# A fused attention and MLP block on one core: the second half's attention moved to a written list of slots, and the attention output loaded with one DMA a tile

## The chip, the cores and the metric

The kernel runs on one core of one Trainium2 chip. The metric is device time in microseconds (us) for one execution; lower is better. A core has a matrix engine (PE, with its weight loads PEld), a vector engine (DVE), a scalar engine (ACT), a GpSimd engine (POOL) and a sync engine (SP) that here issues all DMA transfers. Each engine works through its own instructions strictly in the order of the program, and waits on semaphores for the others.

## The reference

`x` has 2048 tokens of 576 channels. The output is `x + A(LN(x)) + B(LN(x))`, all in float32:

```python
# A: 32 heads of 18 channels, window of 8 keys with stride 2
qkv = xn @ wqkv
logits = q . k[pos - 2*w] * scale        # w = 0..7, masked where pos - 2*w < 0
o = softmax(logits) . v[pos - 2*w]
A = o @ wo
# B: 576 -> 4608 -> 576
B = mish(xn @ w1 + b1) @ w2
```

## The kernel before

**Halves.** The tokens are done in two halves of 1024 (`hf` 0 and 1), of eight tiles of 128 tokens each. Each half goes through LayerNorm and transposes, the q/k/v projection (`q` items, for the second half also `z` items, which use a seven-product scheme), and 18 groups `q` of 256 hidden channels of the MLP. The products are made of float32 parts: a high and a low part of each operand and three matmuls instead of one. At the very end come eight `o` blocks (`wo_part`, L1068), which multiply the attention output of both halves with `wo`, two token tiles at a time, add the rest and store.

**The plan.** All of this is one list, `plan`, of 456 items in a fixed order: `("m", hf, q, part)` are six parts of the first MLP product, `("p", ...)` are parts of the second, `("q", ...)`, `("z", ...)`, `("o", ...)` as above. `before(i, fn)` hangs side work on item `i`: weight loads, splits, attention steps. When the program is written out, each item first emits what lies in `soon` (work that an earlier step put off by one item), then its side work in the order in which it was hung, then what an earlier item left in `pend` (the mish evaluations, L716 to L723), then its own matmuls. Every engine gets its instructions in this order; a list of dependencies at the end of the program pins it.

**One group of the first MLP product** (`m1_part`, L730 on) uses three PSUM banks. Part 3's bank is `cur[3]`: the DVE add at L716 reads it (`rt`), and part 4 then accumulates into the same bank. In the group `q = 0` the order of the parts is 0, 2, 1, 3, 5, 4, and the adds that are kept in `late` (among them `rt`) are emitted in part 5. So part 4 cannot begin before the DVE has done `rt`. In the group `q = 1` the order is 0, 2, 1, 3, then one `z` item, then 4 and 5; there too part 4 waits for an `rt` add.

**Attention** (`attention`, L518) is a generator with 73 steps a half: eight pairs of head units, nine steps a pair, and one last step. Steps 0 to 3 of a pair multiply queries with windowed keys into `pr`; the sum over a head's channels (`L543`, DVE) follows at the next step. Normally the product is done on POOL (L538); for the first pair of the second half it is done on DVE (L534). Step 4 takes the maximum (L557), subtracts it (L559) and leaves the exponential for ACT. Step 5 divides (L567 to L569), and steps 5 to 8 multiply with the values on POOL (L576) and sum on DVE (L582). The step after a pair's last one leaves `o_turn` in `soon`: a DVE transpose (L598) into `oT`, and one item later `o_send`, four SP stores into `o_d[hf]` in DRAM (L605). The first call of the generator, four items ahead of its first step, issues the loads of the first two keys and queries (L491, L500).

**Where the steps stand before.** One formula places the 146 steps of both halves: a list `marks` of places with a `rate` each gives every item a cost, the total is cut into equal parts, and each step goes to the next item that the list `ok` allows.

| step of the second half | item before |
|---|---|
| loads of the first keys and queries | 258 (`m 1 0 3`) |
| pair 0, steps 0, 1, 2, 3, 4, 5 | 262 (`m 1 1 2`), 265 (`z 3 3`), 268 (`m 1 2 0`), 271, 274, 278 |
| pair 1, steps 0 and 5 | 291, 307 |
| pair 2, steps 0 and 5 | 320, 335 |
| pair 3, step 0 | 348 |
| pair 7, steps 3 to 8, and the last step | 419, 421, 423, 425, 427, 428, 429 |

The first half's last two steps stand at items 257 and 260. Items 255 to 260 are the six parts of the group `q = 0` in the order 0, 2, 1, 3, 5, 4, items 261 to 264 the parts 0, 2, 1, 3 of `q = 1`, 265 the `z` item, 266 part 4. Item 270 is the first product with the second MLP weights (`p_item`, L861).

**The end.** `o_load` (L890) fetches a token tile of the attention output into `o`: one DMA of 256 KB for 512 channels (L894), and the remaining 64 channels twice, into the lower and the upper 64 partitions, by two DMAs (L897). Tiles 0 and 1 of the first half are loaded one item ahead of item 428 (`p 1 17 1 0`), tiles 2 and 3 at the first `o` item, 432, the others two blocks ahead of their use. `o_split` (L899) then copies and splits them with ACT (L916 to L932) and DVE (L919 on); `wo_part` calls `o_split` for the next block while it does its own.

Of the kernel before, what the change touches and what calls it, by code (L numbers as in the profile page):

```python
# [8 lines left out]
F32 = mybir.dt.float32  # L9
# [5 lines left out]
S, D, F = 2048, 576, 4608  # L15
H, DH, W, DIL = 32, 18, 8, 2
HALO = (W - 1) * DIL
P = 128
NH = 2
# [3 lines left out]
TJ = SH // P  # L23
JB = TJ // NB
KT = D // P
NF = F // P
NP = NF // 2
NQ = 4
UQ = 4
PU = 2  # L30
CU = 2 * DH
OC = 4
# [7 lines left out]
def block_kernel(ctx: ExitStack, tc: tile.TileContext, x, wq, wo, w1, b1, w2, mask, out):  # L40
    nc = tc.nc
# [5 lines left out]
    dram = ctx.enter_context(tc.tile_pool(name="dram", bufs=1, space=bass.MemoryType.DRAM))  # L47
# [548 lines left out]
    def o_turn(hf, pair, og):  # L596
        oT = sb.tile([P, PU * CU * TJ], F32, tag="oT", bufs=1, name=f"oT_{hf}_{pair}")
        nc.vector.transpose(oT, og.rearrange("p c j -> p (c j)"))  # L598
        soon.append(lambda: o_send(hf, pair, oT))

    def o_send(hf, pair, oT):
        rows = o_d[hf][pair * PU * CU:(pair + 1) * PU * CU].rearrange("(n c) j p -> (c j) n p", c=4)
        for g in range(4):
            part = slice(g * 32, (g + 1) * 32)
            nc.sync.dma_start(rows[:, :, part], oT[part].rearrange("i (n k) -> i n k", k=32))  # L605

    ASTEPS = NQ * UQ // PU * 9

# [281 lines left out]
    def o_load(hf, j):  # L890
        if j >= TJ or (hf, j) in os_:
            return
        o = os_[hf, j] = sb.tile([P, 5 * P], F32, tag="xn", bufs=XNB, name=f"o_{hf}_{j}")
        nc.sync.dma_start(o[:, 0:KT * P].rearrange("p (k t) -> p k t", k=KT),  # L894
                          o_d[hf][0:KT * P, j, :].rearrange("(k p) t -> p k t", p=P))
        for r_ in range(2):
            nc.sync.dma_start(o[r_ * 64:(r_ + 1) * 64, KT * P:], o_d[hf][KT * P:D, j, :])  # L897

    def o_split(p, step, early=False):  # L899
        hf, j = divmod(2 * p, TJ)  # L900
# [234 lines left out]

    kv_d = [dram.tile([2 * UQ, HALO + S, CU], F32, name=f"kv_d{g}") for g in range(NQ)]
    q_d = [dram.tile([UQ, S, CU], F32, name=f"q_d{g}") for g in range(NQ)]
    o_d = [dram.tile([D, TJ, P], F32, name=f"o_d{h}") for h in range(NH)]
    y_d = dram.tile([SH, D], F32, name="y_d")

    def rest_loads():
# [6 lines left out]
    at = {}  # L1148
# [7 lines left out]
    def before(i, fn):  # L1156
        plan[max(i, 0)][1].append(fn)
# [75 lines left out]
    CHUNKS = ((1, 0), (1, 1), (0, 0), (0, 1))  # L1233
# [112 lines left out]
    def spot(hf, q, i):  # L1346
        return at["s", hf, q, i]

    for q in range(NP):
        if q == 0:  # L1350
            i = at["q", 0, 3, 1, 0]
            ps_ = dict(raw=i - 3, sums=i - 1, wa=i, wc=i + 1, t0=i + 2, t1=i + 4)
        elif q == 1:
            i = at["q", 0, 3, 0, 0]
# [16 lines left out]
    for q in range(1, 2 * OC + 1):  # L1371
        i = spot(0, q, (3,2)[q > 1])
# [5 lines left out]
    i = spot(0, NP - 1, 0)  # L1378
# [5 lines left out]
    i = at["q", 1, 0, 1, 1]  # L1384
# [4 lines left out]
    i = spot(0, 9, 4)  # L1389
    for k in range(2):  # L1390
        for n, steps in enumerate((
# [4 lines left out]
            for kind, name in steps:  # L1396
                f = dict(l=z_load, s=z_sum, h=z_high, o=z_low, k=z_keep)[kind]
                d = 30 + 2 * n + (n >= 14) if k else 2 * n if n < 10 else (19, 20, 22, 23, 25, 26, 27)[n - 10]
                before(i + d, lambda f=f, name=name, k=k: f(name, k))
    for q in range(NP):  # L1400
        if q == 0:
            i = at["z", JB - 1, 0]
            ps_ = dict(wa=i - 7, t0=i - 6, t1=i - 5, wc=i - 4)
        elif q == 1:
            i = spot(1, 0, 0)
# [19 lines left out]
    for n, (a, b) in enumerate((("P6", "P1"), ("P7", "P6"), ("P6", "P5"), ("P2", "P1"), ("P3", "P6"), ("P4", "P7"), ("P5", "P7"))):  # L1425
        for pr in range(2):
            i = items[-2][2] + 1 + (0,1,2)[n] if n < 3 else at["p", 1, J + 0 - 1, n > 4, pr] + (1, 7, 1, 2)[n - 3]
# [6 lines left out]
    i = at["q", 0, 1, 1, 0]  # L1434
# [3 lines left out]
    i = at["q", 0, 3, 1, 0]  # L1438
# [5 lines left out]
    i = at["q", 1, 0, 1, 1]  # L1444
    for n in range(8):
        c, k = divmod(n, 4)
# [7 lines left out]
    for n in range(0, JB, 2):  # L1454
        i = at["q", 0, 1, 0, n]
# [4 lines left out]
    for n in range(TJ):  # L1460
        i = spot(0, 2 + n, 2)
# [3 lines left out]
    i = spot(0, NP - 2, 0)  # L1465
# [7 lines left out]
    for n, (name, pr) in enumerate((name, pr) for name in ("P4", "P5", "P2", "P3") for pr in range(2)):  # L1473
        i = items[dict(P4=0, P5=2, P3=2, P2=3)[name]][2] + pr
# [4 lines left out]
    att = {}  # L1479
    T = [0.0]  # L1480
# [1 line left out]
        T.append(T[-1] + p_[2])  # L1482

    ok = [True] * len(plan)
    for hf in range(NH):
        for q in range(1, NP):
            for i in range(10):
                ok[spot(hf, q, i)] = i in ((0, 3, 7, 9), (0, 3, 5, 7, 9))[hf] + (1,) * (hf and q >= NP - 4) and (q > 1 or i)

    for q in range(2 * OC + 2):  # L1490
        for i in range(spot(1, q, 0), spot(1, q, 9) + 1):
            ok[i] = True

    marks = [at["q", 0, 2, 0, 1], at["q", 0, 3, 0, 0], spot(0, 1, 0), spot(0, 2 * OC + 1, 0), at["q", 1, 0, 0, 0], at["z", 0, 0], spot(1, 0, 0),
             spot(1, 2, 0), spot(1, 2 * OC + 2, 0), spot(1, NP - 1, 0), at["o", 0, 0], at["o", 2, 0]]
    rate = (1.15, 0.4, 0.5, 0.8, 1.15, 1.25, 1.2, 0.8, 1.5, 0.8, 0)
    T = [0.0]
    for i in range(len(plan)):
        w = [r_ for m, r_ in zip(marks, rate) if m <= i][-1:] or [0]
        T.append(T[-1] + plan[i][2] * w[0])  # L1500
    total = T[at["o", 2, 0]]
    steps = ASTEPS + 1
    cuts = []
    k = marks[0] - 1
    for n in range(2 * steps):
        t = n * total / (2 * steps)
        if n == steps:
            k = max(k, spot(1, 0, 0) + 1)
        k = next(k for k in range(k + 1, len(plan)) if T[k + 1] > t and ok[k])
        hf = n // steps  # L1510
        if n % steps == 0:
            before(k - 4, lambda hf=hf: (att.__setitem__(hf, attention(hf)), next(att[hf])))
        before(k, lambda hf=hf: next(att[hf], None))
        cuts.append(k)

    i = spot(1, *(11,3))
    for k in range(4):
# [3 lines left out]
    for n, name in enumerate(("T3", "T1", "T2", "T4", "B11", "B21", "B22", "R", "D")):  # L1521
        k = i + 10 + (2, 5, 10, 15, 20, 25, 30, 35, 40)[n]
# [5 lines left out]
    i = spot(1, NP - 1, 0)  # L1528
# [3 lines left out]
    j = at["p", 1, NP - 1, 1, 0]  # L1532
# [2 lines left out]
        before(j + n // 2, lambda name=name: wo_fetch(name))  # L1535
    for k in range(2):
        before(j + -1, lambda k=k: o_load(0, k))
        before(at["o", 0, 0], lambda k=k: o_load(0, 2 + k))
    for k in range(4):
        before(j + (1, 1, 2, 3)[k], lambda k=k: o_split(0, k, True))  # L1540
    for p_ in range(TJ // 2):
# [1 line left out]
    for k in range(4, 2 * TJ):  # L1543
        before(at["o", k // 2 - 2, 0], lambda k=k: o_load(*divmod(k, TJ)))
# [52 lines left out]
```

## Time and profile before

| | |
|---|---|
| median of 3 runs | 1114.85 us (1114.71 to 1118.95) |
| the profiled execution | 1116.75 us |
| its span, first to last instruction | 1115.0 us |
| mean granted PE clock | 0.998 |

The profile is of one execution. A row of the timeline gives the start and the length of a piece in us, the engine, the line of the kernel, the operation, the tiles as output<-input, how many instructions are merged in it, and in brackets the idle time of the engine ahead of it with what ended that. SPq rows are DMAs as SP issues them. A row of the view of waits gives engine, tile and line that waited, what it waited for, the sum in us, how often, and the longest. A row of the view of windows gives a stretch, then for each engine the busy time and the instructions, then the granted PE clock as a share of full speed, the mean busy share of the 16 DMA engines, and GB/s.

### The profile page before, as it was taken

The page shows a single profiled execution, that of the slowest core. Times are in us where ns is not written, and L with a number is a line of the kernel's source. Part 1 is how long each engine was busy: PE and PEld are TensorE (multiplying, and loading weights), DVE is VectorE, ACT ScalarE, POOL GpSimd, SP SyncE. Part 2 cuts the span into 40 slices and gives each one's busy share as a digit, 9 for nine tenths or more (in the row PEclk, how much of TensorE's full clock was granted, in tenths as well). Part 3 has the DMA queues.
Part 4 walks back from the last instruction along what each step waited for, and adds up shares of the span by engine and source line. Part 5 has one row for each costly group of instructions (what it writes and reads, how often), then busy time and mean ns, then how long its engine had stood idle before and what let it go on. Part 6 is the DMA issues. An engine that isn't in the chain of part 4 may idle for free.

```text
span 1115.0 us, 18242 instructions
## 1 busy us (share of the span) xinstructions
PE 1102.7 (99%) x6550; PEld 1015.9 (91%) x6550; DVE 846.0 (76%) x1371; ACT 499.2 (45%) x917; POOL 777.4 (70%) x631
## 2 busy tenths in 40 slices
PE   8999999999999999999999999999999999999998
PEld 7999899999999999999999889988899999998898
DVE  6369788888889888897666576686775677877776
ACT  5544645544554534555232355353342443444253
POOL 2479777767679687785787336666779878877532
PEclk9999999999999999999999999999999999999999
DMA  6899695868767858666697797764665567777474
GB/s 204 281 313 312 229 350 214 293 225 282 260 239 268 272 200 310 245 234 215 190 332 254 230 351 268 238 215 161 217 224 180 193 209 238 278 254 238 138 227 143
DMA packets 174558, 271.08 MB, mean 243 GB/s; under 512 B 49506, under 2 KB 116356, under 8 KB 174468
## 3 DMA queue, kind: packets, MB, share of 16 engines
q1 hardware_dynamic: 174468, 269.91, 71.3%
q8 instruction: 52, 0.85, 0.3%
q14 instruction: 38, 0.31, 0.1%
HBM read 160.39 MB, written 109.48 MB: 242 GB/s over the span
## 4 chain that ended last, share of the span: by engine, by line
PE 87%; POOL 6%; DVE 3%; issue 1%; ACT 1%; DMA 1%; SPq 1%; POOLq 0%; DVEq 0%; ACTq 0%
PE h L671 28%; PE po L769 21%; PE pq L348 9%; PE po L882 9%; PE po L861 7%; PE h L677 5%; PE o L1068 5%; PE z L446 3%; POOL pv L576 2%; POOL act L723 1%; POOL pr L538 1%; POOL s L622 1%; DVE u L815 1%; POOL accP L870 1%; PE ta L75 0%
## 5 line engine op out<-in xcount | busy, mean ns | idle before, releaser
L769 PEld LDWEIGHTS po<-w,act 128*128 128x128 f32 x1728 | 236.4, 188 | 6.0 <-POOL act L723 0.4
L769 PE MATMUL po<-w,act 128*128 128x288 f32 x1728 | 240.7, 295 | 0.1
L576 POOL TENSOR_TENSOR pv<-L,kv 128x576 f32<-128x576 f32 x128 | 177.2, 1482 | 40.6 <-DVE L L569 31.1
L538 POOL TENSOR_TENSOR pr<-q,kv 128x576 f32<-128x576 f32 x120 | 184.6, 1564 | 6.9 <-DMA q<-q_d 5.1
L723 POOL TENSOR_TENSOR act<-c,act 128x512 fp32r<-128x512 f32 x81 | 107.6, 1329 | 114.2 <-ACT act L722 110.9
L773 DVE TENSOR_TENSOR acc<-po,acc 128x288 f32<-128x288 f32 x288 | 119.5, 449 | 29.6 <-PE po L769 28.8
L348 PE MATMUL pq<-wq,xt 128*128 128x432 f32 x672 | 136.4, 361 | 1.0 <-ACT xt L81 0.9
L882 PEld LDWEIGHTS po<-w,act 128*128 128x128 f32 x960 | 130.9, 188 | 5.2 <-DVE accP L885 2.1
L882 PE MATMUL po<-w,act 128*128 128x288 f32 x960 | 133.6, 295 | 1.5 <-DVE accP L885 1.4
L348 PEld LDWEIGHTS pq<-wq,xt 128*128 128x128 f32 x672 | 125.0, 188 | 7.9 <-ACT xt L81 1.5
L717 ACT ACTIVATE c<-c,b1c 128x512 f32<-128x512 f32 x81 | 58.7, 725 | 144.7 <-DVE c L716 144.5
L671 PE MATMUL h<-xt,t 128*128 128x512 f32 x432 | 110.5, 391 | 0.2 <-DVE rt L716 0.2
L671 PE MATMUL h<-S,t 128*128 128x512 f32 x432 | 110.4, 391 | 0.0
L582 DVE TENSOR_REDUCE og<-pv 128x144 f32<-128x1152 f32 x64 | 86.1, 1346 | 29.8 <-POOL pv L576 29.8
L671 PE MATMUL h<-xt,wa 128*128 128x512 f32 x432 | 104.1, 390 | 0.0
L543 DVE TENSOR_REDUCE L<-pr 128x64 f32<-128x1152 f32 x64 | 85.8, 1343 | 23.1 <-POOL pr L538 23.0
L705 ACT COPY c<-h 128x512 f32<-128x512 f32 x81 | 47.5, 586 | 119.2 <-PE h L677 65.8
L671 PEld LDWEIGHTS h<-xt,wa 128*128 128x128 f32 x432 | 80.9, 188 | 17.0
L861 PEld LDWEIGHTS po<-pw,u 128*128 128x128 f32 x672 | 92.1, 188 | 4.4 <-DVE u L815 1.8
L861 PE MATMUL po<-pw,u 128*128 128x288 f32 x672 | 94.1, 295 | 1.4 <-DVE u L815 1.4
L671 PEld LDWEIGHTS h<-xt,t 128*128 128x128 f32 x432 | 79.0, 188 | 15.1 <-DVE rt L716 0.6
L671 PEld LDWEIGHTS h<-S,t 128*128 128x128 f32 x432 | 77.9, 188 | 12.8
(229 smaller groups left out, 1842.9 us busy)
## 6 DMA issues: line engine op xcount, KB each, us to landing
kv<-kv_d SPq DMA_DIRECT2D x64, 396.0 KB, 5.2
kept_t<-t SPq DMA_DIRECT2D x36, 512.0 KB, 4.8
t<-kept_t SPq DMA_DIRECT2D x36, 512.0 KB, 4.7
rw<-in_w SPq DMA_DIRECT2D x36, 320.0 KB, 4.6
kept_wa<-wa SPq DMA_DIRECT2D x18, 640.0 KB, 4.6
kept_w<-w SPq DMA_DIRECT2D x20, 576.0 KB, 4.2
wa<-kept_wa SPq DMA_DIRECT2D x18, 640.0 KB, 4.8
w<-kept_w SPq DMA_DIRECT2D x20, 576.0 KB, 4.7
```

The costliest lines, as they stand in the source:

```text
L348: nc.tensor.matmul(pq[:, 0:432], XT[:, xi, tok], wt[wi][:, hl, 0:432], start=i == 0, stop=i == len(seq) - 1)
L538: nc.gpsimd.tensor_tensor(out=pr[:, x:x + hh], in0=q[:, j0 + x:j0 + x + hh, None, :].to_broadcast([P, hh, W, CU]), in1=win(kt, 0, CU, j0 + ...
L543: nc.vector.tensor_reduce(L[:, k, j0:j0 + hj].rearrange("p j w h -> p (j w h)"), pr.rearrange("p j w (h d) -> p (j w h) d", h=2), axis=AX, ...
L576: nc.gpsimd.tensor_tensor(out=pr[:, x:x + hj].rearrange("p j d w -> p j w d"), in0=L[:, k, x:x + hj, :, h:h + 1].to_broadcast([P, hj, W, DH]),
L582: nc.vector.tensor_reduce(og[:, c0:c0 + DH, :].rearrange("p d j -> p j d"), pr, axis=AX, op=ALU.add)
L671: nc.tensor.matmul(ph, wt[:, wl, wk * P:(wk + 1) * P], X[:, xs, :], start=first and i == 0, stop=last and i == len(seq) - 1, skip_group_ch ...
L717: nc.scalar.activation(t, ph if fresh else t, AF.Mish, bias=b1c[:, f:f + 1])
L723: nc.gpsimd.tensor_tensor(out=a[:, 1, :], in0=t, in1=a[:, 0, :].bitcast(F32), op=ALU.subtract)
L769: nc.tensor.matmul(po, acts[hf, q, b, j][:, al, tok], done["w2", hf, 2 * q + j][:, wl, c * HC:(c + 1) * HC], start=i == 0, stop=i == 5)
L773: nc.vector.tensor_tensor(out=t, in0=po, in1=t, op=ALU.add)
L861: nc.tensor.matmul(po, units[e, k, qq][:, al, tok], w[:, qq, wl, :], start=i == 0, stop=i == 5)
L882: nc.tensor.matmul(po, acts[hf, q, b, j][:, al, tok], done["w2", hf, 2 * q + j][:, wl, c * HC:(c + 1) * HC], start=i == 0, stop=i == 5)
```

## The change

1. `o_d[hf]` gets 640 rows in place of 576. When the last pair of a half is sent, `o_send` stores its last 64 channels a second time into rows 576 to 639: eight stores in place of four for pair 7 of each half.
2. `o_load` is one DMA of 128 partitions by 5 by 128 in place of three.
3. Tiles 2 and 3 of the first half are loaded at item 429 in place of 432.
4. The formula now places the first half only, with the same results but for its last two steps, which go to items 256 and 257. The second half's steps stand in a written list `early`, and every second slot in the last eight groups.

| step of the second half | item before | item after |
|---|---|---|
| loads of the first keys and queries | 258 | 255 |
| pair 0, step 0 | 262 | 259 |
| steps 1, 2, 3, 4, 5, 6 | 265, 268, 271, 274, 278, 281 | 261, 262, 263, 264, 266, 268 |
| steps 7 and 8 | 284, 287 | 271, 274 |
| pair 1, steps 0 and 5 | 291, 307 | 278, 294 |
| pair 2, steps 0 and 5 | 320, 335 | 307, 323 |
| pair 3, step 0 | 348 | 335 |
| pair 7, step 3 to the last | 419 to 429 | the same |

From item 266 to item 345 the steps use the slots that they used before, about four steps of the generator earlier.

```diff
     def o_send(hf, pair, oT):
-        rows = o_d[hf][pair * PU * CU:(pair + 1) * PU * CU].rearrange("(n c) j p -> (c j) n p", c=4)
-        for g in range(4):
-            part = slice(g * 32, (g + 1) * 32)
-            nc.sync.dma_start(rows[:, :, part], oT[part].rearrange("i (n k) -> i n k", k=32))
+        c0, c1 = pair * PU * CU, (pair + 1) * PU * CU
+        for lo, to in ((c0, c0), *(((KT * P, D),) if c1 == D else ())):
+            rows = o_d[hf][to:to + c1 - lo].rearrange("(n c) j p -> (c j) n p", c=4)
+            for g in range(4):
+                part = slice(g * 32, (g + 1) * 32)
+                nc.sync.dma_start(rows[:, :, part],
+                                  oT[part, (lo - c0) * TJ:].rearrange("i (n k) -> i n k", k=32))
...
-        nc.sync.dma_start(o[:, 0:KT * P].rearrange("p (k t) -> p k t", k=KT),
-                          o_d[hf][0:KT * P, j, :].rearrange("(k p) t -> p k t", p=P))
-        for r_ in range(2):
-            nc.sync.dma_start(o[r_ * 64:(r_ + 1) * 64, KT * P:], o_d[hf][KT * P:D, j, :])
+        nc.sync.dma_start(o.rearrange("p (k t) -> p k t", k=5), o_d[hf][:, j, :].rearrange("(k p) t -> p k t", p=P))
...
-    o_d = [dram.tile([D, TJ, P], F32, name=f"o_d{h}") for h in range(NH)]
+    o_d = [dram.tile([5 * P, TJ, P], F32, name=f"o_d{h}") for h in range(NH)]
...
+    last_steps = [spot(1, 0, i) for i in (0, 2, 4)]
+    cuts = [[], []]
     k = marks[0] - 1
-    for n in range(2 * steps):
-        t = n * total / (2 * steps)
-        if n == steps:
-            k = max(k, spot(1, 0, 0) + 1)
+    for n in range(steps - len(last_steps)):
+        t = 6.111 * n
         k = next(k for k in range(k + 1, len(plan)) if T[k + 1] > t and ok[k])
...
+        cuts[0].append(k)
+    cuts[0] += last_steps
+    early = {0: (8,), 1: (0, 2, 4, 6, 8), 2: (0, 3, 6), 3: (0, 3, 6), 4: (0, 4, 7), 5: (0, 3, 7), 6: (1, 4, 7),
+             7: (0, 4, 7), 8: (1, 4, 8), 9: (1, 3, 7)}
+    for q in range(NP):
+        cuts[1] += [spot(1, q, i) for i in early.get(q, (1, 3, 5, 7, 9))]
+        if q == 2 * OC:
+            cuts[1].append(at["p", "x", OC - 1, 4])
+    cuts[1] = sorted(set(cuts[1])) + [at["p", 1, NP - 1, *c] for c in CHUNKS]
+    cuts[1] = cuts[1][:steps]
...
-        before(at["o", 0, 0], lambda k=k: o_load(0, 2 + k))
+        before(j + 1, lambda k=k: o_load(0, 2 + k))
```

More of the change, by code (lines that the diff above doesn't have):

```diff
@@ L1484, in block_kernel @@
     ok = [True] * len(plan)
[L1485 to L1496, printed above, removed]
+    for q in range(1, NP):
+        for i in range(10):
+            ok[spot(0, q, i)] = i in (0, 3, 7, 9) and (q > 1 or i)
+    marks = [at["q", 0, 2, 0, 1], at["q", 0, 3, 0, 0], spot(0, 1, 0), spot(0, 2 * OC + 1, 0), at["q", 1, 0, 0, 0],
+             at["z", 0, 0], spot(1, 0, 0)]
+    rate = (1.15, 0.4, 0.5, 0.8, 1.15, 1.25, 0)
     T = [0.0]
@@ L1500, in block_kernel @@
         T.append(T[-1] + plan[i][2] * w[0])
-    total = T[at["o", 2, 0]]
     steps = ASTEPS + 1
-    cuts = []
+    last_steps = [spot(1, 0, i) for i in (0, 2, 4)]
+    cuts = [[], []]
     k = marks[0] - 1
-    for n in range(2 * steps):
-        t = n * total / (2 * steps)
-        if n == steps:
-            k = max(k, spot(1, 0, 0) + 1)
+    for n in range(steps - len(last_steps)):
+        t = 6.111 * n
         k = next(k for k in range(k + 1, len(plan)) if T[k + 1] > t and ok[k])
[L1510 to L1514, printed above, removed]
+        cuts[0].append(k)
[8 more added lines that the diff above has]
+    cuts[1] = cuts[1][:steps]
+    assert len(cuts[0]) == len(cuts[1]) == steps, (len(cuts[0]), len(cuts[1]), steps)
+    for hf in range(NH):
+        before(cuts[hf][0] - 4, lambda hf=hf: (att.__setitem__(hf, attention(hf)), next(att[hf])))
+        for k in cuts[hf]:
+            before(k, lambda hf=hf: next(att[hf], None))
     i = spot(1, *(11,3))
```

## The prediction

> **What bounds the kernel now.** The page comes first: it says which engine has room at all.
>
> ```profile
> span 1115.0 us, 18242 instructions
> PE 1102.7 (99%) x6550; PEld 1015.9 (91%) x6550; DVE 846.0 (76%) x1371; ACT 499.2 (45%) x917; POOL 777.4 (70%) x631
> ```
>
> PE is busy for 1102.7 of 1115.0 us. The change adds no matmul and takes none away, and PE's order stays as it is. So the most that it can win is PE's idle time of 12.3 us, and whatever holds up a matmul is lost. The second view is that of PE's waits: the rows that lie in the second half.
>
> ```profile
> PE o L1068 <- ACT ot L932: 2.0, 1, 2.0
> PE po L861 <- DVE u L815: 1.4, 2, 0.8
> PE h L671 <- DVE rt L716: 0.2, 1, 0.2
> PE po L882 <- DVE accP L885: 1.4, 2, 1.0
> ```
>
> The longest is one wait of 2.0 us in the `o` blocks. The third view is the timeline around it.
>
> ```profile
> 1048.64 0.77 DVE L598 STREAM_TRANSPOSE oT<-og 128x576 f32<-128x576 f32 x1
> 1049.44 1.98 SPq L605 DMA_DIRECT2D o_d<-oT  x4
> 1054.04 2.95 SPq L897 DMA_DIRECT2D o<-o_d  x2
> 1057.60 0.43 PE L1068 MATMUL o<-wo_r,ob 128*128 128x288 f32 x2
> 1058.40 0.38 ACT L916 COPY ot<-o 128x256 f32<-128x256 f32 x1 [5.78 <-DMA o<-o_d]
> 1058.81 0.43 DVE L919 TENSOR_TENSOR s<-ot,o 128x256 f32<-128x256 f32 x1 [2.13 <-ACT ot L916]
> 1059.49 0.81 DVE L1072 TENSOR_TENSOR y<-o,y 128x288 f32<-128x288 f32 x2
> 1060.04 1.31 PE L1068 MATMUL o<-wo,oS 128*128 128x288 f32 x6 [2.01 <-ACT ot L932]
> ```
>
> SP sends the last attention output at 1049.44, as soon as the transpose before it ends. The six DMAs for tiles 2 and 3 stand behind those stores; SP is done with them at 1054.04 + 2.95 = 1056.99. ACT waits 5.78 us for the data, until 1058.40. The DVE's split (L919) waits for ACT, and behind it in the DVE's queue stands the add (L1072) that empties the PSUM bank which PE needs. So the name in PE's row, ACT L932, is not the cause; the late load is. Then the view of windows:
>
> ```profile
> 1060.00:1064.00 4.00, 3.96 (x18) 3.99 (x19) 2.72 (x7) 1.48 (x4) 1.27 (x1) 0.57 1.07 309
> 1064.00:1068.00 4.00, 4.00 (x32) 4.00 (x31) 2.82 (x8) 2.19 (x6) 1.30 (x1) 1.00 0.78 271
> ```
>
> In the 4 us after the stop PE's granted clock is 0.57, and 18 matmuls get done against 32 in the next 4 us. That costs 0.43 x 4 = 1.7 us more. The stop is worth 2.0 + 1.7 = 3.7 us in all.
>
> **The change, part by part.**
>
> *Tiles 2 and 3 loaded at item 429, one DMA a tile.* In the changed kernel's order on SP these two DMAs stand ahead of the first `y` load and ahead of the stores of `oT`; in the profile that place is here, and the landing time of the output loads is below it.
>
> ```profile
> 1040.02 0.32 SPq L1043 DMA_DIRECT2D y<-y_d  x1
> DMA to landing us min/median/max: 2.1/2.9/7.9
> ```
>
> Issued near 1040.0 and landed within 7.9 us, the data is there by 1048, before the first `o` block. ACT is free and the copy can run as soon as the last MLP banks are emptied. Nothing else stands between the L1072 add and its matmul, which is over by 1057. What is late next is the matmul itself, so PE goes on at 1057.60 + 0.43 = 1058.03. I take the full **-3.7 us**; 0 is the other end.
>
> *The other loads and the stores.* The `o_load` DMAs go from 48 to 16, the stores from 64 to 72. No wait of PE in the `o` blocks names another of these loads, so I count 0. The four more stores at the end cost SP about as long again as the row at 1049.44, 1.98 us, and behind them stands only the second `y` load, which is issued earlier than now because the six DMAs are gone.
>
> *The early steps.* Here is the price. In the timeline of the stretch where the second half's attention will begin (items 255 to 266):
>
> ```profile
> 626.94 2.48 POOL L576 TENSOR_TENSOR pv<-L,kv 128x576 f32<-128x576 f32 x2 [2.41 <-DVE og L582]
> 628.72 3.84 SPq L282 DMA_DIRECT2D t<-kept_t  x2
> 632.66 0.37 SPq L491 DMA_DIRECT2D kv<-kv_d  x1
> 633.08 0.42 SPq L500 DMA_DIRECT2D q<-q_d  x1
> 633.33 0.69 DVE L716 TENSOR_TENSOR rt<-h,rt 128x512 f32<-128x512 f32 x1 [5.20 <-ACT rt L705]
> 634.53 1.34 DVE L582 TENSOR_REDUCE og<-pv 128x144 f32<-128x1152 f32 x1
> 635.31 1.55 PE L671 MATMUL h<-xt,t 128*128 128x512 f32 x6
> 635.91 0.78 DVE L598 STREAM_TRANSPOSE oT<-og 128x576 f32<-128x576 f32 x1
> 646.43 1.66 PE L671 MATMUL h<-xt,t 128*128 128x512 f32 x6
> ```
>
> The row at 633.33 is the `rt` add that part 4 of group 0 (PE, 635.31) needs, and 646.43 is part 4 of group 1. The DVE sat idle for 5.20 us ahead of `rt`. Into that hole the changed order puts three things ahead of `rt`: the sum L582, the transpose L598, and the first product L534 of the second half. The first two fit: POOL ends at 629.42, so they are done at 629.42 + 1.34 + 0.78 = 631.54. The product must wait for its key and query. Their loads now go out between the two `t` loads of the row at 628.72, and the DMA engines are full there:
>
> ```profile
> 625.00:635.00 10.00, 9.33 (x41) 7.36 (x40) 4.80 (x7) 3.44 (x5) 2.48 (x2) 1.00 1.05 314
> DMA to landing us min/median/max: 4.7/4.7/4.7
> ```
>
> The second row is for the query loads around 633: the first landed at 633.08 + 4.7 = 637.8. With full engines the only thing that the new order takes out of its way is one `t` load of 512 KB, at 314 GB/s 1.6 us. So the query lands at S = 637.8 - 1.6 = **636.2**. Bounds: 631.5, when the DVE is free, if it landed that soon; 637.8, if nothing is gained.
>
> From S the DVE's queue in the changed order is: product, `rt`, `ra`, sum, product, `rm`, sum, product, `ra`, sum, product, L803, sum, L557, L559, and then the `rt` add of group 1, for which part 4 of group 1 waits. The prices are the steps from start to start of these rows:
>
> ```profile
> 640.60 0.69 DVE L716 TENSOR_TENSOR ra<-h,ra 128x512 f32<-128x512 f32 x1 [1.29 <-PE h L677]
> 641.21 0.68 DVE L803 TENSOR_TENSOR rm<-ra,rm 128x512 f32<-128x512 f32 x1
> 641.81 1.34 DVE L543 TENSOR_REDUCE L<-pr 128x64 f32<-128x1152 f32 x1
> 643.07 1.35 DVE L534 TENSOR_TENSOR pr<-q,kv 128x1152 f32<-128x1152 f32 x1
> 663.57 1.34 DVE L543 TENSOR_REDUCE L<-pr 128x64 f32<-128x1152 f32 x1
> 664.94 0.42 DVE L557 TENSOR_REDUCE m<-L 128x32 f32<-128x256 f32 x1
> 665.39 0.42 DVE L559 TENSOR_TENSOR L<-L,m 128x256 f32<-128x256 f32 x1
> 665.74 0.68 DVE L716 TENSOR_TENSOR rt<-h,rt 128x512 f32<-128x512 f32 x1
> ```
>
> L716 takes 0.61, L803 0.60, L543 1.26, and L534, equally long, 1.26; a sum with L557 right behind it 1.37, L557 0.45, L559 0.35. The first `rt` is done at S + 1.26 + 0.69 = 638.1. So PE, ready at 635.31, stops for **2.8 us**. The whole queue is 4 x 1.26 + 3 x 1.26 + 1.37 + 0.45 + 0.35 + 4 x 0.61 + 0.60 + 0.68 = 14.7 us, so the `rt` of group 1 is done at S + 14.7 = 650.9. PE needs 646.43 - 635.31 - 0.2 (the wait in the row of `rt` above) = 10.9 us from one part 4 to the next; it would be there at 649.0 and waits again, for 1.9 us. Against 646.43 that is a loss of 650.9 - 646.4 = **4.5 us**. The first stop, longer than the 2.0 us above, should bring the reduced clock as well; its 1.7 us fall almost all into the second wait, since PE then arrives at 650.7. I add 0.5 for the `rm` and `ra` adds, which themselves wait for PE's slowed parts. Early loss: **5.0 us**; it can be 0 (S = 631.5) and at most 6.1 + 1.7 = 7.8 (S = 637.8, and a reduced clock behind the second wait too).
>
> What waits behind the blocked product, beside the adds: ACT's mish (L717), which needs `rt`, and through the bank `ra` part 0 of group 1; both are inside the 14.7 us. POOL has no share in this stretch until the values are multiplied. On SP the eight stores and the loads of the values now stand ahead of `pw` and later weights, each some 10 us ahead of its use; I count 0.
>
> *Items 266 to 345.* The same slots hold other kinds of steps. The waits there, 1.4 us at L815, are of the size of one late DVE add; the mix of sums, products and divisions is the same, only dealt to other items. I take 0, with -1.4 and +3 as ends. From 346 on the steps stand up to ten items earlier and about as densely; the only PE waits there are the two at L882, 1.4 us, and they lie beside the steps at 419 to 429, which keep their places. I count 0.
>
> **The sum.** 5.0 - 3.7 + 0 = +1.3 us. The sum is made against the profiled execution (1116.75 us, span 1115.0); the median before is 1114.85 us, and I put the difference on the median: **1116.2 us**. A measurement of this kernel can tell about 0.5%, 5.6 us, from no change, so this is no change: a gain at the end paid for at the start.
>
> **The rivals.**
>
> *A, the early loads come in time.* The DVE's hole is real, and the stores that fill the DMA engines may drain sooner. With S = 632 the first stop is gone and the DVE is done with the second `rt` at 646.7: loss 0.3, sum -3.4, **1111.5 us**. Against it: a full queue in the row of 625 to 635. If the waits at L815 went too (-1.4) and others with them, it would pass below 1109.3.
>
> *B, slower: the DVE does not get free.* After the dense steps POOL multiplies the values (steps 5 and 6, items 266 and 268) beside the DVE's adds L803 and L815, where POOL now does almost nothing. A DVE add of two SBUF operands beside a POOL one is slow elsewhere:
>
> ```profile
> 744.75 1.79 DVE L815 TENSOR_TENSOR u<-rm,u 128x512 fp32r<-128x512 f32 x1
> ```
>
> That is 1.79 against 0.68 for L803 above, 1.1 more. Three such adds stand ahead of the second operand of item 270. By my count it comes just in time, so each slow one counts: 3 x 1.1 = 3.3 us, and a reduced clock for another 1.7. Sum 1.3 + 5.0 = +6.3, **1121.2 us**. It decides from the point where the DVE runs more than about 0.1 us behind PE at item 270.
>
> *C, the end keeps its stop.* If the split waits for something else, as the PSUM bank, the 3.7 us stay: +5.0, **1119.9 us**. For it: PE's row names ACT. Against it: ACT's idle row names the DMA.
>
> *D, the clock has its own rule.* If the reduced clock at 1060 did not come from the 2.0 us stop, its 1.7 us stay wherever they fall, and the early stop costs itself alone: 4.5 - 2.0 = +2.5, **1117.4 us**. The Trainium skill, "TensorE: Matmul & The Clock Gate", Part 1, gives such a rule: the clock is halved after an idle window of about 3.4 us, whose phase is free. By it neither 2.0 nor 2.8 us would be enough. This trace does not agree: 2.0 us were followed by 0.57.
>
> **How the numbers follow.** Forecast 0.45, with its own range 1113.5 to 1118.5 (S between 635 and 637); A 0.22; B 0.18; C 0.08; D 0.07. Below 1109.3 lies a third of A: faster 0.07. Above 1120.4 lie B and a part of C: slower 0.22. The rest, 0.71, is within 0.5%. The range from 1110.0 to 1122.0 leaves out about 2 in 10: the far end of A, and of B where the clock falls twice.
>
> **What would show it.** Right: in the changed profile PE stops for 2 to 3 us ahead of part 4 of group 0 with the DVE's `rt` as releaser, and again ahead of part 4 of group 1; the granted clock falls in the first of these places and no longer at 1060; L1068 has no wait of 2 us. Wrong: the first L534 starts before 633 (A); PE waits for L815 at item 270 (B); ACT L916 still waits for `o_d`, or L1068 still stops (C); a stop over 2 us with a clock of 1.00 behind it (D).

## The result, and the profile after

| | before | after |
|---|---|---|
| median (lowest to highest) of 15 runs each | 1115.22 us (1114.60 to 1118.95) | 1120.16 us (1117.96 to 1121.95) |
| profiled execution: time, span, clock | 1116.75, 1115.0, 0.998 | 1118.50, 1116.6, 1.000 |

After over before is 1.0037, with an interval from 1.0030 to 1.0045 (the two medians alone stand 1.0044 apart). That is slower, and within the 0.5% that the prediction called no change. The forecast was 1116.2 us, so it was 4.0 us too low; 1120.16 lies inside its range of 1110.0 to 1122.0.

The page of after and its view of PE's waits, against those of before:

```profile
span 1116.6 us, 18199 instructions
PE 1102.1 (99%) x6550; PEld 1014.6 (91%) x6550; DVE 853.3 (76%) x1371; ACT 499.6 (45%) x917; POOL 780.1 (70%) x631
```

```profile
PE h L674 <- DVE rt L719: 4.3, 3, 3.0
...
PE po L885 <- DVE accP L888: 1.0, 1, 1.0
PE po L864 <- ACT u L812: 0.8, 1, 0.8
...
PE po L864 <- DVE u L818: 0.4, 1, 0.4
```

PE does the same 6550 matmuls, and its busy time is the same within 0.6 us. The row of 2.0 us at L1068 is gone, and the wait for `rt` has grown from 0.2 us in one piece to 4.3 us in three. (Lines of after stand 3 further down than in before: L719 is L716.) First the end, in the timeline and then in the windows of after:

```profile
1044.69 1.00 SPq L897 DMA_DIRECT2D o<-o_d  x2
...
1054.80 4.29 SPq L607 DMA_DIRECT2D o_d<-oT  x8
...
1058.31 0.38 ACT L916 COPY ot<-o 128x256 f32<-128x256 f32 x1 [0.33 <-DVE accP L888]
...
1063.22 0.97 PE L1068 MATMUL o<-wo,oS 128*128 128x288 f32 x6
```

```profile
1058.00:1062.00 4.00, 4.00 (x32) 4.00 (x31) 2.44 (x7) 1.67 (x5) 1.29 (x1) 1.00 0.81 162
1062.00:1066.00 4.00, 4.00 (x32) 4.00 (x31) 3.29 (x10) 1.37 (x3) 0.18 (x1) 1.00 1.02 338
```

The two loads now go out ten microseconds ahead of the stores. ACT's copy at L916 no longer waits for a DMA, and PE does 32 matmuls in each 4 us at a clock of 1.00. Then the beginning of the second half's attention, and ahead of it the first matmuls of item 255 in both kernels, which say how far the two timelines are shifted. This row is before's:

```profile
624.73 2.93 PE L671 MATMUL h<-xt,wa 128*128 128x512 f32 x12
```

and these are after's:

```profile
625.36 2.93 PE L674 MATMUL h<-xt,wa 128*128 128x512 f32 x12
...
631.47 0.78 DVE L598 STREAM_TRANSPOSE oT<-og 128x576 f32<-128x576 f32 x1
631.88 0.42 SPq L500 DMA_DIRECT2D q<-q_d  x1
...
634.12 7.12 SPq L607 DMA_DIRECT2D o_d<-oT  x8
...
637.09 1.36 DVE L534 TENSOR_TENSOR pr<-q,kv 128x1152 f32<-128x1152 f32 x1 [4.85 <-DMA q<-q_d]
638.37 0.69 DVE L719 TENSOR_TENSOR rt<-h,rt 128x512 f32<-128x512 f32 x1
...
639.11 1.66 PE L674 MATMUL h<-xt,t 128*128 128x512 f32 x6 [3.00 <-DVE rt L719]
...
651.13 0.68 DVE L719 TENSOR_TENSOR rt<-h,rt 128x512 f32<-128x512 f32 x1
...
651.87 1.65 PE L674 MATMUL h<-xt,t 128*128 128x512 f32 x6 [1.00 <-DVE rt L719]
```

After runs 625.36 - 624.73 = 0.63 us later before anything has changed. The DVE is done with its transpose at 632.25 and then stands for 4.85 us in front of the first product, until the query lands. The `rt` add stands behind the product, so PE stops for 3.00 us ahead of part 4 of group 0, and for 1.00 us more ahead of part 4 of group 1. That matmul was at 646.43 and is now at 651.87: 5.44 less the shift of 0.63 is a loss of **4.8 us**.

One thing does not show in these two traces, because the profiled run of each kernel is of its rarer kind: the clock. Of 53 runs of before made beside the experiments, 41 had a mean granted clock of 1.000 (spans 1112.7 to 1114.1) and 12 had 0.998 (1114.6 to 1115.5). The profiled one is one of the latter. Of after's 15 runs, three had 1.000 (1116.1 to 1116.6, the profiled one among them), four 0.998 (1117.5 to 1118.2) and eight 0.997 (1118.3 to 1120.1). So at a full clock the change costs 1116.3 - 1113.3 = 3.0 us, and in most runs, some 1118.6 against 1113.3, about 5.

### The profile page after: what moved, and what is told of

Same layout as the page of the kernel before. It is cut to its first block, busy times and chain, and to the rows that moved or that the text cites. A ratio compares the mean times of both kernels' runs of the same rounds, so it can differ in the third digit from the quotient of the medians.

```text
span 1116.6 us, 18199 instructions
## 1 busy us (share of the span) xinstructions
PE 1102.1 (99%) x6550; PEld 1014.6 (91%) x6550; DVE 853.3 (76%) x1371; ACT 499.6 (45%) x917; POOL 780.1 (70%) x631
## 4 chain that ended last, share of the span: by engine, by line
PE 89%; DVE 4%; POOL 3%; DMA 2%; ACT 1%; issue 1%; SPq 0%; DVEq 0%; POOLq 0%; ACTq 0%
PE h L674 28%; PE po L772 20%; PE po L885 11%; PE pq L348 9%; PE po L864 7%; PE h L680 5%; PE o L1068 5%; PE z L446 3%; POOL pv L576 1%; DMA acc<-in_x 1%; POOL s L625 1%; DVE rm L806 1%; POOL act L726 1%; DVE L L543 1%; DMA t<-kept_t 1%
## 5 line engine op out<-in xcount | busy, mean ns | idle before, releaser
L888 DVE TENSOR_TENSOR accP<-po,accP 128x288 f32<-128x288 f32 x160 | 69.0, 453 | 29.8 <-PE po L885 28.2
```

The lines of the kernel that those rows point to most:

```text
L888: nc.vector.tensor_tensor(out=t, in0=po, in1=t, op=ALU.add)
```

## The experiments

The theory behind the runs, called Q in the texts below: the late key and query hold up the DVE's queue, which costs about 5 us, and the end wins its stop of 2.0 us. Its rivals: the loss sits at the end, in the stores and the loads (E); it comes from the steps dealt to other items from 266 on (P); only the product ahead of the first `rt` costs anything (F); the load on the DVE alone is to blame (G). S says that the extra stores of the first half hold up SP. Four kernels were run beside 27 runs of before (median 1115.22 us), four more beside 26 runs of it (1115.38 us).

| kernel | median us (lowest to highest) | over before | mean clock of its runs |
|---|---|---|---|
| e1 loads and stores alone | 1114.25 (1113.19 to 1115.02) | 0.9988 [0.9979, 0.9997] | 1.000 in 11 of 11 |
| e2 steps alone | 1121.32 (1119.82 to 1125.13) | 1.0059 [1.0044, 1.0073] | 1.000 in 2, 0.998 in 2, 0.995 in 2 |
| e3 after, keys loaded 3 items earlier | 1114.42 (1113.98 to 1114.80) | 0.9990 [0.9982, 0.9999] | 1.000 in 11 of 11 |
| e4 after, first step one item later | 1118.18 (1117.17 to 1119.11) | 1.0026 [1.0016, 1.0035] | 1.000 in 3, 0.998 in 6 |
| e5 e1, extra stores of the first half later | 1112.61 (1112.46 to 1113.42) | 0.9973 [0.9962, 0.9983] | 1.000 in 6, 0.999 in 1 |
| e6 after, products on POOL | 1118.57 (1118.28 to 1119.23) | 1.0025 [1.0014, 1.0035] | 0.998 in 8 of 8 |
| e7 e3, extra stores of the first half later | 1114.42 (1113.91 to 1114.89) | 0.9987 [0.9978, 0.9996] | 1.000 in 11 of 11 |
| e8 before, tiles 2 and 3 loaded at item 429 | 1113.24 (1112.81 to 1114.01) | 0.9980 [0.9971, 0.9988] | 1.000 in 11 of 11 |

**e1, the loads and stores alone.** The old formula places the steps of both halves, and parts 1 to 3 of the change stay (against after):

```diff
-    for n in range(steps - len(last_steps)):
-        t = 6.111 * n
+    for n in range(2 * steps):
+        t = n * total / (2 * steps)
+        if n == steps:
+            k = max(k, spot(1, 0, 0) + 1)
...
-    cuts[0] += last_steps
-    early = {0: (8,), 1: (0, 2, 4, 6, 8), ...}
```

> The old places of all attention steps, with the new loads and stores of the attention output alone. Theory Q (the vector engine's queue behind the early key loads loses about 5 us, and the end wins the stop of 2.0 us, with the reduced clock behind it only where it falls): the stop at L1068 is gone, no other PE wait changes, the time is 2.0 us below the kernel before, up to 3.7 where the runs of the kernel before show a clock below 1.000, and this kernel's granted clock is 1.000 in nearly every run. Rival E (the loss sits at the end, in the eight stores and the other loads): the time is at or above that of the kernel before.

The gain was 1.0 us, where Q gave 2.0; E, no gain at all, does not hold. The stop at L1068 was gone and no run had a reduced clock, but a new stop, which Q did not have, stood elsewhere. The timeline of e1:

```profile
638.17 8.20 SPq L607 DMA_DIRECT2D o_d<-oT  x8
...
656.79 0.44 SPq L846 DMA_DIRECT2D accP<-in_x  x1
...
664.14 0.82 DVE L870 TENSOR_TENSOR accP<-po,accP 128x288 f32<-128x288 f32 x2 [2.04 <-DMA accP<-in_x]
...
665.96 0.82 DVE L870 TENSOR_TENSOR accP<-po,accP 128x288 f32<-128x288 f32 x2 [1.00 <-DMA accP<-in_x]
...
668.88 0.68 DVE L719 TENSOR_TENSOR rt<-h,rt 128x512 f32<-128x512 f32 x1
...
669.61 1.66 PE L674 MATMUL h<-xt,t 128*128 128x512 f32 x6 [1.29 <-DVE rt L719]
```

The same rows in the timeline of before:

```profile
638.25 3.58 SPq L605 DMA_DIRECT2D o_d<-oT  x4
...
652.34 0.49 SPq L843 DMA_DIRECT2D accP<-in_x  x1
```

The first half has the four extra stores too. The prediction counted them at 0 by the weights that stand behind them, and did not name this load of `in_x`. SP takes 8.20 us for the eight in place of 3.58 for four; the first load of `in_x`, which stands behind them on SP, goes out 4.45 us later, the DVE waits for it, `rt` is late again and PE stops for 1.29 us.

**e5, the same without that.** The four extra stores of the first half go out at item 278:

```diff
-        for lo, to in ((c0, c0), *(((KT * P, D),) if c1 == D else ())):
+        def part_(lo, to):
...
+        part_(c0, c0)
+        if c1 == D and hf == 0:
+            before(278, lambda: part_(KT * P, D))
+        elif c1 == D:
+            part_(KT * P, D)
```

> The kernel e1_loads_only, with the four extra stores of the first half's last pair moved from item 261 to item 278, behind the loads of the first accumulator tiles. Theory S (in e1_loads_only those four stores hold SP for some 4 us, the accumulator tiles land late, and PE stops for 1.3 us ahead of part 4 of group 2 and 0.4 us before): both stops go, 1.3 to 1.8 us below e1_loads_only, about 1112.7. Rival: the stop comes from elsewhere, 1114.2 as before.

1112.61 us, as S gave, which is 0.9973 against e1's 0.9988: 0.0015, or 1.7 us, was the price of where those stores stood. The two intervals overlap a little, so the size is rough, but the stop in question is gone. Its view of PE's waits has neither the stop for `rt` nor the one at L1068 (the lines stand 5 further down than in after):

```profile
PE po L890 <- DVE accP L893: 1.4, 2, 1.0
...
PE po L869 <- DVE u L823: 1.2, 2, 0.8
...
PE h L679 <- DVE rt L724: 0.2, 1, 0.2
```

This is the version with the lowest median, 2.8 us (0.27%) ahead of before; the interval of e8, next, overlaps with its.

**e8, the end's stop alone.** Before with one line changed, still three DMAs a tile and no extra stores:

```diff
-        before(at["o", 0, 0], lambda k=k: o_load(0, 2 + k))
+        before(j + 1, lambda k=k: o_load(0, 2 + k))
```

> The kernel before with one difference: the loads of tiles 2 and 3 stand at item 429 in place of 432, still three DMAs a tile, and no extra store. Theory Q and S: the stop of 2.0 us at L1068 is gone and nothing is paid for it, 2.0 us below the kernel before, 1113.2, and the granted clock is 1.000 in all runs. Rival: the stop is bound to the single DMA a tile (six DMAs take 5.5 us of SP): it stays over 1 us, 1114 or more.

It gained 2.1 us, the stop and little more: between runs at a full clock alone, the spans differ by 1113.3 - 1111.4 = 1.9. It is not 3.7 because the reduced clock belongs to 12 of 53 runs of before only; the medians hold almost none of it. What else it changes is that none of its eleven runs has it. With three DMAs a tile still in place, the earlier place of the loads alone removed the stop.

**e2, the steps alone.** Before with part 4 of the change:

```diff
+    last_steps = [spot(1, 0, i) for i in (0, 2, 4)]
...
+    early = {0: (8,), 1: (0, 2, 4, 6, 8), ...}
...
+    cuts[1] = sorted(set(cuts[1])) + [at["p", 1, NP - 1, *c] for c in CHUNKS]
```

> The new places of the attention steps with the old loads and stores. Theory Q: the stops of about 3.0 and 1.0 us ahead of the two parts 4 as in the changed kernel, and the stop of 2.0 us at L1068 back: 2.0 to 3.7 us above the changed kernel, 7 us above the kernel before. Rival E: at or below the changed kernel.

The median is 1.2 us above after's, where Q gave 2.0 to 3.7. Its two runs at full clock have spans of 1117.9 and 1118.0 us, 1.7 more than after's 1116.3. So the end's gain looks about as large in company of the early loss as alone. Two of its six runs have a mean clock of 0.995, lower than any of after's, and one of these was profiled. Rows of e2's timeline, then of its windows and its waits:

```profile
638.63 2.93 PE L671 MATMUL h<-xt,t 128*128 128x512 f32 x6 [3.19 <-DVE rt L716]
...
642.45 0.69 DVE L716 TENSOR_TENSOR rm<-h,rm 128x512 f32<-128x512 f32 x1 [0.75 <-PE h L677]
...
646.82 0.69 DVE L716 TENSOR_TENSOR ra<-h,ra 128x512 f32<-128x512 f32 x1 [1.16 <-PE h L677]
...
653.47 1.65 PE L671 MATMUL h<-xt,t 128*128 128x512 f32 x6 [0.66 <-DVE rt L716]
```

```profile
638.00:642.00 4.00, 3.37 (x8) 2.73 (x9) 3.69 (x4) 1.91 (x3) 0.00 (x0) 0.50 0.89 204
640.00:644.00 4.00, 4.00 (x11) 3.09 (x10) 3.25 (x4) 1.24 (x2) 0.00 (x0) 0.50 0.93 274
```

```profile
PE po L861 <- ACT rm L717: 2.4, 1, 2.4
PE o L1068 <- ACT ot L932: 1.7, 1, 1.7
```

Here is what after's own trace missed: behind the stop of 3.19 us the granted clock is 0.50, and six matmuls take 2.93 us where after's six, at 639.11, take 1.66. The DVE's adds `rm` and `ra` then wait 0.75 and 1.16 us for PE's slow parts, the second `rt` comes later by that, and part 4 of group 1 begins at 653.47. The stop of 2.4 us, at 824.61, belongs neither to the early loss nor to the end: a DVE add just ahead of it took 4.47 us, and in after's trace no such stop exists. Whether e2's other runs have it is not known, so the 1.7 us above may hold a part of it.

**e3, the first keys and queries three items earlier.** After with their loads at item 252:

```diff
-        before(cuts[hf][0] - 4, lambda hf=hf: ...)
+        before(cuts[hf][0] - (4, 7)[hf], lambda hf=hf: ...)
```

> The changed kernel with one difference: the loads of the second half's first keys and queries are hung on item 252 in place of 255, ahead of the stores of the last z items and of the weights for group 1. Theory Q: the first product L534 starts near 631.5, when the vector engine is free, both stops go to under 0.5 us, and the time falls by 5 us and by what the reduced clock took, to 1113 to 1114, 1 to 2 us below the kernel before. Rival P (the loss is made by the steps dealt to other items from 266 on, and the early stops are made good later): within 1 us of the changed kernel, about 1120.

1114.42 us, just above the 1113 to 1114 that Q gave, or 0.9990 against after's 1.0037: 5.2 us by these ratios, 5.7 between the medians. The DVE's and PE's rows in the timeline of e3:

```profile
631.85 1.31 DVE L534 TENSOR_TENSOR pr<-q,kv 128x1152 f32<-128x1152 f32 x1
...
633.64 0.69 DVE L719 TENSOR_TENSOR rt<-h,rt 128x512 f32<-128x512 f32 x1 [0.47 <-ACT rt L708]
...
635.62 1.55 PE L674 MATMUL h<-xt,t 128*128 128x512 f32 x6
...
646.83 0.68 DVE L719 TENSOR_TENSOR rt<-h,rt 128x512 f32<-128x512 f32 x1
...
647.57 1.66 PE L674 MATMUL h<-xt,t 128*128 128x512 f32 x6 [0.67 <-DVE rt L719]
```

The product starts about 5 us earlier and has no wait for a DMA; part 4 of group 0 follows without a stop. The queue from the product to the end of the second `rt`, 15.7 us here, is still there and costs 0.67 us, with its data in time. Only the loads were moved, so the late data were the cause of the early loss, as Q says; P, no change, does not hold.

**e4, the first step one item later,** behind the blocked `rt` add, with the loads still at item 255:

```diff
-    early = {0: (8,), 1: (0, 2, 4, 6, 8), 2: ...
+    early = {0: (9,), 1: (0, 2, 4, 6, 8), 2: ...
...
-        before(cuts[hf][0] - 4, lambda hf=hf: ...)
+        before(cuts[hf][0] - (4, 5)[hf], lambda hf=hf: ...)
```

> The changed kernel with the first step of pair 0 one item later, at 260 in place of 259, so that the adds rt and ra stand ahead of the first product in the vector engine's queue; the key loads stay at item 255. Theory Q: the first stop is gone, but the rest of the queue (four products, four sums, about 13.5 us from the landing of the query) still stands ahead of the second rt, so PE stops once, for about 3.3 us, ahead of part 4 of group 1: about 1.2 us below the changed kernel, 1119. Rival F (only the product ahead of the first rt costs anything): no stop over 0.5 us, 4 us below the changed kernel, 1116 or less.

2.0 us below after, where Q gave 1.2, and by another way. Only 0.5 us of it shows at a full clock (spans of 1115.7 against 1116.2); the rest is clock. From e4's view of PE's waits:

```profile
PE h L674 <- ACT ra L708: 2.1, 1, 2.1
PE po L864 <- DVE u L818: 1.6, 1, 1.6
```

F, no stop over 0.5 us, does not hold, and the one stop of 3.3 us ahead of part 4 that Q forecast did not come either. The stop went from `rt` to the next bank: the DVE was still blocked in front of its product, now at 636.72, `rm` behind it came late, ACT's next copy stood behind ACT's use of `rm`, and PE stopped for 2.1 us ahead of part 2 of group 1. That a step is moved behind the add that PE waits for doesn't help while the engine's next step still waits for a DMA.

**e6, the products on POOL.** After with one line changed, so that a late key blocks POOL and not the DVE:

```diff
-                    on = hf and pair == 0
+                    on = False
```

> The changed kernel with the products of the second half's first pair on POOL (L538) in place of the vector engine (L534), as in all other pairs. Theory Q: the first stop goes, since no product stands ahead of the first rt any more; but four POOL products of 3.1 us each from the landing near 637, then a sum, the maximum and the subtraction, still stand ahead of the second rt, so part 4 of group 1 begins near 652 as in the changed kernel, after one stop of about 4.5 us: 1119 to 1121, within 1 us of the changed kernel. Rival G (the vector engine's load alone is to blame, and POOL, idle in that stretch, takes it over for nothing): no stop over 1 us, 1115 or less.

1118.57 us, 0.4 below the lower end that Q gave; G, 1115 or less, does not hold. The timeline of e6:

```profile
636.45 11.62 POOL L538 TENSOR_TENSOR pr<-q,kv 128x576 f32<-128x576 f32 x8 [7.20 <-DMA q<-q_d]
...
642.53 1.66 PE L674 MATMUL h<-S,t 128*128 128x512 f32 x6 [2.21 <-ACT ra L708]
...
651.03 2.48 PE L674 MATMUL h<-xt,t 128*128 128x512 f32 x6 [2.04 <-DVE rt L719]
```

The wait for the query is now POOL's, as POOL's 7.20 us say. But the DVE's sum waits for POOL's product, and the adds behind the sum wait with it: the block came back one engine further on, as two stops of 2.2 and 2.0 us, where Q forecast one of 4.5. All eight runs had a clock of 0.998; in the profiled one the first stop left the clock alone, and behind the second six matmuls took 2.48 us.

**e7, both repairs,** e3 with the extra stores of the first half at item 276:

```diff
-        before(cuts[hf][0] - 4, lambda hf=hf: ...)
+        before(cuts[hf][0] - (4, 7)[hf], lambda hf=hf: ...)
...
+            before(276, lambda: part_(KT * P, D))
```

> The kernel e3_keys_earlier with the four extra stores of the first half's last pair moved to item 276. In e3_keys_earlier no wait behind those stores shows in PE's waits, so theory S says no change: 1114.4 within 0.5. If the stores cost something wherever they stand ahead of the weights, 1 us less.

1114.42 us, the same as e3. In the changed order, here with the keys at item 252, the stores stand elsewhere on SP and moving them changes nothing, so there the "I count 0" was right. e3 and e7 stay 1.8 us behind e5. The waits of PE in the second half of e3, but for one of 0.7 us that both kernels have, are these:

```profile
PE po L885 <- DVE accP L888: 1.0, 1, 1.0
PE h L674 <- DVE rt L719: 1.0, 2, 0.7
PE po L864 <- ACT u L812: 0.8, 1, 0.8
PE po L864 <- DVE u L818: 0.8, 1, 0.8
PE h L674 <- DVE c L719: 0.3, 1, 0.3
```

They add up to 3.9 us against 2.8 in e5's rows above. That is 1.1 of the 1.8 us; what makes the rest stays open.

## Why the prediction was right or wrong

The forecast was 4.0 us too low. 1120.16 lies outside the range that the forecast gave for itself, 1113.5 to 1118.5, and within 1110.0 to 1122.0, which had been widened for its rivals; that the number fell inside is in part luck.

**The early loss: right in its mechanism and place, 4.8 us for 4.5, at a full clock.** The query landed at 637.09 - 0.63 = 636.5 (forecast 636.2). From there to the end of the second `rt`, at 651.81, the DVE took 14.72 us (forecast 14.7). The stops were 3.0 and 1.0 us (forecast 2.8 and 1.9); in this run the clock stayed at 1.00, and the second stop was shorter because parts between the two began later, by 0.1 to 0.2 us each. The prediction's list of waits in the second half leaves out one row, 0.7 us at L671 for ACT's `rt`; after has the same 0.7, so nothing hangs on it.

**Where the 4.0 us went: the clock, at both ends, in opposite directions.** The step that failed is "the sum is made against the profiled execution ..., and I put the difference on the median". The tail's 3.7 us were the stop, 2.0, and the reduced clock, 1.7, of an execution that had it. In 41 of 53 runs, and so in the median, before doesn't have it; e8 puts the term at **2.1 us** on the median. And "the first stop ... should bring the reduced clock as well; its 1.7 us fall almost all into the second wait" was half right: 12 of 15 runs of after have a reduced clock, but there it isn't hidden. The term that was too small is the 0.5 us for the `rm` and `ra` adds that wait for PE's slowed parts: in e2's trace these two waits are 0.75 + 1.16 = **1.9 us**, and part 4 of group 1 begins 7.1 us later than in before (653.47 against 646.43, with a shift of -0.04), against 4.8 in after's trace at a full clock. On after's times the clock is worth about as much: its three runs at a full clock have a median of 1117.99 us, all fifteen 1120.16, so **2.2 us**. The early steps cost 4.8 + 2.2 = 7.0 in place of 5.0. So 1116.2 + 1.6 at the tail + 2.0 early + 0.4 (the median of before moved from 1114.85 to 1115.22 with more runs) is 1120.2, against 1120.16 measured.

**Stores and other loads, 0: right for the new order, with a gap in the reason.** e7 shows 0 in the new order. In the old order the same stores cost 1.7 us (e1 against e5), through a load of `in_x` that stood behind them on SP. The prediction's reason, that what stands behind them has some 10 us to spare, named the weights and not this load.

**Items 266 on, 0: about right.** In after's waits `u` at L818 has 0.4 us in place of 1.4 at L815, and two rows for `u` from ACT and `accP` are 0.8 and 1.0. Nothing large came or went.

**The rivals.** A, the loads in time, did not happen, but e3 shows what it was worth: 1114.4 us, and not 1111.5, of which 1.6 is the tail priced too high again and 0.4 the median of before; the second `rt` is 0.67 us late and not 0.3, and the rest is open. B, the DVE not free at item 270: the three adds are slow, 1.37, 1.61 and 1.18 us in after's trace, but they cost 0.43 us in the row of L818, where 3.3 were thought possible (1.60 in e4). C, the end keeps its stop: no. That the numbers of C, 1119.9, and of B, 1121.2, lie nearest to the measured one is luck, since neither happened at its size. D, the clock has its own rule: its number, 1117.4, was 2.8 us too low, nearer than the forecast. Its sign came in after's profile, a stop of 3.00 us with a clock of 1.00 behind it, and the forecast's sign, a clock that falls there, did not. But 12 of 15 runs have a reduced clock: D's idea, that a stop doesn't bring it for certain, is what the runs show. That it doesn't come from the stop at L1068 they don't bear out: with that stop gone, e8 has it in none of eleven runs.

## What to carry to other kernels

When a step is put into an engine's idle time, ask first when its data land, and not how long it takes: in a queue kept in order, a step that waits 4.85 us for a DMA costs that to every add behind it, and moving the wait to another engine (e6) or one place on (e4) only moves the stop. The same holds for SP: four more small stores delayed a load 4.45 us further on. And a gain read from one profiled execution must be checked against what most runs do: a term that hangs on the granted clock is a chance times a price, not a price, and here neither was the same at every stop.

## What the runs showed of the hardware

Stops of PE of about 2 us and more brought a reduced clock in a part of the runs, shorter ones hardly ever. With no stop above 1.3 us in the second half, 44 of 44 runs (e1, e3, e7, e8) had a mean clock of 1.000, and six of e5's seven, the other 0.999. With before's stop of 2.0 us it was reduced in 12 of 53, with e4's 2.1 us (and one of 1.6) in 6 of 9, with e6's two stops of 2.2 and 2.0 us in 8 of 8, with after's 3.0 and 1.0 us in 12 of 15, with e2's 3.2, 2.4 and 1.7 us in 4 of 6. The stops are read from one profile of each kernel, and from 2 us up the counts do not simply follow the length: in e6's profile it was the shorter of the two that was followed by slow matmuls. The price in before is the 1.7 us of the prediction: its runs at 0.998 have spans about 1.75 us longer than those at 1.000. It is not the same elsewhere: about 1 us in e4, and 2.7 us for after's runs at 0.997. In e2's trace the clock stood at 0.50 from 638 to 644, longer than the 0.43 x 4 / 0.5 = 3.4 us of before. The Trainium skill, "TensorE: Matmul & The Clock Gate", Part 1, says that the clock is halved after an idle window of about 3.4 us, and that this window runs freely, so that the moment varies from run to run. The variation agrees with these counts, and the size with before's: by an estimate from that page, half the clock for 3.4 us loses 1.7 us. That a whole window must be idle does not agree: 2.0 us were enough in 12 of 53 runs.

Small stores took SP longer where the DMA engines were full. In after the eight stores of `oT` took SP 7.12 us at the start of the half and 4.29 us at the end; the windows around the two have a mean busy share of the DMA engines of 1.00 and of 0.55:

```profile
634.00:641.00 7.00, 4.00 (x16) 2.99 (x17) 3.91 (x5) 3.13 (x4) 0.00 (x0) 1.00 1.00 293
1054.00:1059.00 5.00, 5.00 (x40) 5.00 (x40) 4.57 (x12) 1.35 (x5) 2.08 (x2) 1.00 0.55 85
```

Two places of one trace do not show that the full DMA engines are the cause.
